# Linear attention on one core: q loaded, transposed and stored for two heads at a time, with fewer buffers and new instruction orders

## The chip, the cores and the metric

The kernel runs on one core of a Trainium2 chip. The core has five engines that run their own instruction streams and meet only at semaphores: TensorE (PE, matrix products and transposes), VectorE (DVE), ScalarE (ACT), GpSimd (POOL) and SyncE (SP), which here issues the transfers. Sixteen DMA engines move the data between memory and the on-chip SBUF; TensorE writes its results into PSUM. The metric is the time of one execution on the device in microseconds, lower is better. Before the change it is 169.24 us, the median of three runs (169.21 to 169.28).

## The reference

There are 32 heads; q, k and v of each are 2048 rows of 128 elements in bf16.

```python
phi_q = where(q > 0, q + 1, exp(q)) + 1e-6
phi_k = where(k > 0, k + 1, exp(k)) + 1e-6
kv  = einsum("bhsd,bhse->bhde", phi_k, v)      # 128 x 128 a head
z   = einsum("bhsd->bhd", phi_k)
num = einsum("bhqd,bhde->bhqe", phi_q, kv)
den = einsum("bhqd,bhd->bhq", phi_q, z) + 1e-6
out = num / den
```

Each head reads 1.5 MB and writes 0.5 MB, so the kernel moves 64 MB (67.1 million bytes).

## The kernel before

A head's 2048 rows lie on 128 partitions, 16 consecutive rows on each (`rows`, line 268). One load of q, k or v is therefore 128 partitions of 16 x 128 bf16 elements, 4,096 contiguous bytes a partition, 512 KB in all. The kernel keeps NI = 7 buffers each for k, q and v, and NO = 16 buffers for the output (line 14). A load may be issued when the operations that read its buffer for the head before (seven heads earlier) are done; the final scaling of a head may be written when the store of the head 16 before has landed.

The feature map is written as min(exp(x), 1) + 1e-6 plus max(x, 0), in two separate tensors that are summed by the matrix product. The steps of head h, by the names that the orders use:

- `ldk`, `ldq`, `ldv` (line 340): the loads, all on SP's queue but the first of v, which ACT issues.
- `ek` (ACT, line 366) and `em` (DVE clamp, line 344): min(exp(k), 1) + 1e-6. `rk` (POOL, line 351; DVE for the first heads): max(k, 0). `v1` (POOL, line 376; DVE at the start): v copied beside a column of ones.
- `kv` (PE, line 383): 32 products of 128 rows by 129 columns, the sum over all rows of the head; `kvs` (DVE, line 355) copies the result to SBUF.
- `T` (PE, line 393): 16 transposes of 128 by 128 into the one PSUM tile `xT`, in two halves. `eq` (ACT, line 397), `emq` (DVE, line 344), `rqa` (ACT, line 349, the first `NA[h]` of the 16 tiles) and `rqb` (DVE, line 350, the others): the same map for q, out of PSUM. The next head's T waits for all readers of `xT`.
- `n` (PE, lines 415 to 422): 32 products and a few small ones, numerator and denominator, in two groups (`n.0` 12 tiles, `n.1` 4 tiles). `a`, `r` (DVE, lines 435, 438) form the reciprocal, and `f` (DVE, line 442) scales group by group into an output buffer.
- `st` (SP, line 450): the store. For most heads it is one transfer of 128 partitions. The stores of head 12 (`ROWS`) and of head 14 (`HALF`) are split into unequal pieces by partitions, 51, 64 and 13, and 68, 60 and 128.

No loop sets the order at run time. The five lists in `ORDER` (lines 97 to 161) give, engine by engine, the order in which all steps of all heads stand; `Program.resolve` (line 199) derives from each step's dependencies the semaphore waits that are still needed. In the middle of the kernel PE's list repeats `kv(h) n(h-1).0 T(h+1) n(h-1).1`, ACT's repeats `ek(h+1) eq(h) rqa(h)`, and POOL does `rk` and `v1` of head h + 2 after `kv(h)`, since `rk`, `v1` and `em` have two buffers each. SP's list mixes loads and stores; SP issues strictly in that order, so a step that has to wait holds back everything behind it in the list. The transfers that are already issued go on meanwhile.

Of the kernel before, what the change touches and what calls it, by code (L numbers as in the profile page):

```python
# [6 lines left out]
P = 128  # L7
# [4 lines left out]
ON = {"rk0.0": "DVE", "rk0.1": "DVE", "rk1.0": "DVE", "v10.1": "DVE", "v11.0": "DVE", "rk2.0": "DVE", "v12.0":  # L12
      "DVE", "rk3.0": "DVE", "v13.0": "DVE"}
NI, NO, NE, NR, NV, NQ, NK = 7, 16, 2, 2, 2, 2, 2
WARM = (2, 8, 4, 1, 1, 1, 1, 1, 1, 1)
HALVES = ((0, 8), (8, 16))
WHOLE = ((0, 16),)

# [9 lines left out]
def ldk_parts(h):  # L28
    return WHOLE

# [12 lines left out]
NA = (8, 8, 8, 8, 8, 8, 8, 8, 8, 8, 8, 8, 8, 8, 8, 8, 8, 8, 8, 8, 8, 8, 8, 8, 8, 8, 8, 8, 8, 8, 14, 16)  # L43


def na(h):
    return NA[h] if h else 0

# [7 lines left out]
HALF = {14: ((0, 68), (68, 128))}  # L56
ROWS = {12: ((0, 51), (51, 115), (115, 128))}
# [29 lines left out]
def rqb_parts(h):  # L87
# [4 lines left out]
    if h == NH - 1:  # L92
# [6 lines left out]
        w3 w9 w7 T0.1 T0.0 w5 w2 w1 T1.0 T1.1 kv0.0 w0 kv0.1 w4 w8 w6 kv1.0 n0.0 T2.1 T2.0 n0.1 kv2.0 n1.0  # L99
        T3.1 n1.1 T3.0 kv3.0 n2.0 T4.1 n2.1 T4.0 kv4.0 n3.0 T5.1 n3.1 T5.0 kv5.0 n4.0 T6.1 T6.0 n4.1 kv6.0  # L100
        n5.0 T7.0 n5.1 T7.1 kv7.0 n6.0 T8.1 T8.0 n6.1 kv8.0 n7.0 T9.0 T9.1 n7.1 kv9.0 n8.0 T10.0 T10.1 n8.1
        kv10.0 n9.0 T11.0 T11.1 n9.1 kv11.0 n10.0 T12.0 T12.1 n10.1 kv12.0 n11.0 T13.0 T13.1 n11.1 kv13.0
        n12.0 T14.0 T14.1 n12.1 kv14.0 n13.0 T15.0 T15.1 n13.1 kv15.0 n14.0 T16.0 T16.1 n14.1 kv16.0 n15.0
        T17.0 T17.1 n15.1 kv17.0 n16.0 T18.0 T18.1 n16.1 kv18.0 n17.0 T19.0 T19.1 n17.1 kv19.0 n18.0 T20.0
        T20.1 n18.1 kv20.0 n19.0 T21.0 T21.1 n19.1 kv21.0 n20.0 T22.0 T22.1 n20.1 kv22.0 n21.0 T23.0 T23.1
        n21.1 kv23.0 n22.0 T24.1 T24.0 n22.1 kv24.0 n23.0 T25.1 T25.0 n23.1 kv25.0 n24.0 T26.0 T26.1 n24.1
        kv26.0 n25.0 T27.1 T27.0 n25.1 kv27.0 n26.0 T28.1 T28.0 n26.1 kv28.0 n27.0 T29.1 T29.0 n27.1 kv29.0
        n28.0 T30.0 T30.1 n28.1 kv30.0 n29.0 n29.1 T31.0 kv31.0 T31.1 n30.0 n30.1 n31.0 n31.2 n31.1
    """,
    "DVE": """  # L110
        ones rk0.0 rk0.1 rqb0.1 rqb0.0 v10.1 em0.0 v1ones0 v1ones1 eps0 em0.1 rk1.0 emq0.1 emq0.0 eps2 em1.0
        eps1 v11.0 kvs0 emq1.0 rqb1.0 rk2.0 v12.0 rk3.0 em2.0 r0.0 kvs1 f0.0 em3.0 v13.0 a0.1 kvs2 r0.1
        rqb2.0 f0.1 r1.0 f1.0 emq2.0 em4.0 a1.1 rqb3.0 r1.1 kvs3 f1.1 r2.0 f2.0 emq3.0 em5.0 a2.1 rqb4.0
        r2.1 kvs4 f2.1 r3.0 f3.0 emq4.0 em6.0 a3.1 r3.1 rqb5.0 f3.1 r4.0 kvs5 f4.0 emq5.0 em7.0 a4.1 rqb6.0
        r4.1 kvs6 f4.1 r5.0 f5.0 emq6.0 em8.0 a5.1 rqb7.0 r5.1 kvs7 f5.1 r6.0 f6.0 emq7.0 em9.0 a6.1 kvs8
        r6.1 rqb8.0 f6.1 r7.0 f7.0 emq8.0 em10.0 a7.1 rqb9.0 r7.1 f7.1 r8.0 kvs9 f8.0 emq9.0 em11.0 a8.1
        r8.1 rqb10.0 f8.1 r9.0 kvs10 f9.0 emq10.0 em12.0 a9.1 r9.1 rqb11.0 f9.1 r10.0 kvs11 f10.0 emq11.0
        em13.0 a10.1 r10.1 rqb12.0 f10.1 r11.0 kvs12 f11.0 emq12.0 em14.0 a11.1 r11.1 rqb13.0 f11.1 r12.0
        kvs13 f12.0 emq13.0 em15.0 a12.1 r12.1 rqb14.0 f12.1 r13.0 kvs14 f13.0 emq14.0 em16.0 a13.1 r13.1
        rqb15.0 f13.1 r14.0 kvs15 f14.0 emq15.0 em17.0 a14.1 r14.1 rqb16.0 f14.1 r15.0 kvs16 f15.0 emq16.0  # L120
        em18.0 a15.1 r15.1 rqb17.0 f15.1 r16.0 kvs17 f16.0 emq17.0 em19.0 a16.1 r16.1 rqb18.0 f16.1 r17.0
        kvs18 f17.0 emq18.0 em20.0 a17.1 r17.1 rqb19.0 f17.1 r18.0 kvs19 f18.0 emq19.0 em21.0 a18.1 r18.1
        rqb20.0 f18.1 r19.0 kvs20 f19.0 emq20.0 em22.0 a19.1 r19.1 rqb21.0 f19.1 r20.0 kvs21 f20.0 emq21.0
        em23.0 a20.1 r20.1 rqb22.0 f20.1 r21.0 kvs22 f21.0 emq22.0 em24.0 a21.1 rqb23.0 r21.1 kvs23 f21.1
        r22.0 f22.0 emq23.0 em25.0 a22.1 r22.1 rqb24.0 f22.1 r23.0 kvs24 f23.0 emq24.0 em26.0 a23.1 kvs25
        r23.1 rqb25.0 f23.1 r24.0 f24.0 emq25.0 em27.0 a24.1 rqb26.0 r24.1 f24.1 r25.0 kvs26 f25.0 emq26.0
        em28.0 a25.1 kvs27 r25.1 rqb27.0 f25.1 r26.0 f26.0 emq27.0 em29.0 a26.1 r26.1 rqb28.0 f26.1 r27.0
        kvs28 f27.0 emq28.0 em30.0 a27.1 r27.1 rqb29.0 f27.1 r28.0 kvs29 f28.0 emq29.0 a28.1 kvs30 r28.1
        f28.1 em31.0 rqb30.0 r29.0 emq30.0 f29.0 a29.1 kvs31 emq31.0 r29.1 f29.1 emq31.1 emq31.2 r30.0 f30.0
        a30.1 r30.1 f30.1 r31.2 r31.0 f31.2 a31.1 f31.0 r31.1 f31.1  # L130
    """,
    "ACT": """
        exp ldv0.0 ek0.1 eq0.1 eq0.0 ek0.0 ek1.0 eq1.0 ek2.0 rqa1 ek3.0 eq2.0 rqa2 ek4.0 eq3.0 rqa3 ek5.0
        eq4.0 rqa4 ek6.0 eq5.0 rqa5 ek7.0 eq6.0 rqa6 ek8.0 eq7.0 rqa7 ek9.0 eq8.0 rqa8 ek10.0 eq9.0 rqa9
        ek11.0 eq10.0 rqa10 ek12.0 eq11.0 rqa11 ek13.0 eq12.0 rqa12 ek14.0 eq13.0 rqa13 ek15.0 eq14.0 rqa14
        ek16.0 eq15.0 rqa15 ek17.0 eq16.0 rqa16 ek18.0 eq17.0 rqa17 ek19.0 eq18.0 rqa18 ek20.0 eq19.0 rqa19
        ek21.0 eq20.0 rqa20 ek22.0 eq21.0 rqa21 ek23.0 eq22.0 rqa22 ek24.0 eq23.0 rqa23 ek25.0 eq24.0 rqa24
        ek26.0 eq25.0 rqa25 ek27.0 eq26.0 rqa26 ek28.0 eq27.0 rqa27 ek29.0 eq28.0 rqa28 ek30.0 eq29.0 rqa29
        ek31.0 rqa30 eq30.0 eq31.0 eq31.1 eq31.2 rqa31
    """,  # L140
    "POOL": """
        ident0 ident v10.0 rk4.0 v14.0 rk5.0 v15.0 rk6.0 v16.0 rk7.0 v17.0 v18.0 rk8.0 rk9.0 v19.0 rk10.0
        v110.0 v111.0 rk11.0 v112.0 rk12.0 v113.0 rk13.0 v114.0 rk14.0 v115.0 rk15.0 v116.0 rk16.0 rk17.0
        v117.0 rk18.0 v118.0 v119.0 rk19.0 v120.0 rk20.0 rk21.0 v121.0 rk22.0 v122.0 v123.0 rk23.0 v124.0
        rk24.0 rk25.0 v125.0 rk26.0 v126.0 rk27.0 v127.0 rk28.0 v128.0 rk29.0 v129.0 rk30.0 v130.0 rk31.0
        v131.0
    """,
    "SP": """
        ldq0.0 ldk0.0 ldq1.0 ldk1.0 ldk3.0 ldv1.0 ldk2.0 ldv2.0 ldq2.0 ldv3.0 ldk4.0 ldq3.0 ldv4.0 ldk5.0
        ldq4.0 ldv5.0 ldq5.0 ldk6.0 ldk7.0 ldv6.0 ldq6.0 ldv7.0 ldq8.0 ldq7.0 ldv8.0 ldk8.0 ldk9.0 ldk11.0  # L150
        ldk10.0 ldv9.0 ldv10.0 ldq9.0 ldv14.0 ldq10.0 ldk13.0 ldv11.0 ldv12.0 ldq11.0 ldk12.0 ldq13.0
        ldk14.0 ldv13.0 ldq12.0 ldk15.0 ldq14.0 st1.0 ldk16.0 ldk18.0 ldv19.0 ldv15.0 ldq15.0 ldq16.0
        ldk17.0 ldq17.0 ldv16.0 ldk19.0 ldv18.0 ldv17.0 st3.0 ldk20.0 st0.0 ldq20.0 ldq21.0 ldq18.0 ldv20.0
        st12.0 ldk21.0 ldv21.0 st7.0 ldq19.0 ldk22.0 ldk23.0 st2.0 ldv23.0 ldq22.0 ldv22.0 ldk26.0 ldv25.0
        st4.0 ldv24.0 ldk25.0 ldq23.0 ldv26.0 ldk24.0 st5.0 st6.0 ldq27.0 ldq24.0 st10.0 ldk28.0 ldq25.0
        ldk27.0 st8.0 ldq26.0 ldq29.0 ldv27.0 st9.0 ldv28.0 ldk29.0 ldq28.0 st22.0 st12.2 ldv29.0 ldv30.0
        ldk30.0 st11.0 ldq30.0 st14.1 ldk31.0 st12.1 st15.0 ldv31.0 ldq31.0 st18.0 st13.0 st20.0 st14.2
        st17.0 st16.0 st14.0 st21.0 st26.0 st23.0 st27.0 st25.0 st24.0 st29.0 st19.0 st28.0 st30.0 st31.0
# [99 lines left out]
def bass_standalone__linear_attn_elu__prompt_kernel(nc: bass.Bass, q: bass.AP, k: bass.AP, v: bass.AP, out: bass.AP):  # L258
# [11 lines left out]
    with ExitStack() as es:  # L270
# [11 lines left out]
        k_sb, q_sb, v_sb = (sb([P, NI, NT, D]) for _ in range(3))  # L282
# [15 lines left out]

        def over(name, h, parts, t0, t1):
            return [f"{name}{h}.{i}" for i, (a, b) in enumerate(parts(h)) if a < t1 and t0 < b]  # L300
# [4 lines left out]
        def freed(n, h, *names):  # L305
            return [d for name, parts in names for d in every(name, h - n, parts)] if h >= n else []
# [4 lines left out]

        def rqs(h, t0=0, t1=NT):
            return ([f"rqa{h}"] if t0 < na(h) else []) + over("rqb", h, rqb_parts, t0, t1)
# [25 lines left out]
        def load(name, dst, src, h, i, t0, t1, last):  # L339
            add("ACT" if f"ld{name}{h}.{i}" in BY_ACT else "SP", f"ld{name}{h}.{i}", lambda e: e.dma_start(dst[:, h % NI, t0:t1], rows(src, h)[:, t0:t1]),  # L340
                last, dma=f"{name}{h % NI}.{i}")
# [15 lines left out]
        def head(h):  # L357
            for i, (a, b) in enumerate(ldk_parts(h)):
                load("k", k_sb, kf, h, i, a, b, freed(NI, h, ("ek", k_parts), ("rk", k_parts)))
            for i, (a, b) in enumerate(ld_parts(h)):  # L360
                load("q", q_sb, qf, h, i, a, b, freed(NI, h, ("T", t_parts)))
            for i, (a, b) in enumerate(ld_parts(h)):
                load("v", v_sb, vf, h, i, a, b, freed(NI, h, ("v1", v_parts)) if h else ["ident"])
# [133 lines left out]
```

## Time and profile before

| | before |
|---|---|
| median of three runs | 169.24 us |
| the profiled execution: its own time | 169.41 us |
| its span, first to last instruction | 168.1 us |
| granted TensorE clock | 0.988 |
| PE, DVE, ACT, POOL busy | 155.7, 155.8, 149.4, 84.4 us |
| read from memory, written to memory | 50.33 MB, 16.78 MB |
| mean DMA rate over the span | 402 GB/s |

The busy time of an engine is the sum over its instructions, with overlaps counted once; matrix products and the weight loads that overlap them (PEld) are counted apart. The span is shorter than the execution's own time, which has start and end around it (1.31 us in this execution). The slices divide the span into 40 parts of 4.2 us; a digit 9 is 90% or more. The DMA share is the mean over the sixteen DMA engines; as their packets overlap a little, it can pass 1.

### The profile page before, as it was taken

What the parts mean: (1) busy time and instruction counts of PE and PEld (TensorE: products, weight loads), DVE (VectorE), ACT (ScalarE), POOL (GpSimd) and SP (SyncE); (2) the same over time, 40 slices, a digit from 0 to 9 for tenths busy, and PEclk for the clock granted to TensorE, in tenths of its full rate; (3) what the DMA queues carried; (4) which work ended last, traced back from release to release, by engine and by line L of the source; (5) the groups of instructions that cost most, each with busy time, mean ns of one, the idle gap of its engine ahead of it and who ended that gap; (6) DMA issues with size and microseconds to landing.
All of it is one profiled execution on the core that took longest, in us unless ns stands there. A gap on an engine that the chain in (4) does not pass through costs nothing.

```text
span 168.1 us, 6169 instructions
## 1 busy us (share of the span) xinstructions
PE 155.7 (93%) x2709; PEld 150.8 (90%) x2709; DVE 155.8 (93%) x309; ACT 149.4 (89%) x101; POOL 84.4 (50%) x63
## 2 busy tenths in 40 slices
PE   3999999999999999999599999999999999999650
PEld 1689999999999999999589999999999999999640
DVE  0499999999999999999999999999999999999971
ACT  3799999999999999999669999999999999997600
POOL 1100355566666666546926667676555566670000
PEclk9999999999999999999999999999999999999995
DMA  5999999999999999999999999999999999999996
GB/s 212 409 420 414 401 407 411 401 409 406 407 409 403 408 411 417 407 406 416 406 421 414 418 412 408 421 412 416 414 415 416 414 417 411 415 415 414 375 406 243
DMA packets 18910, 67.51 MB, mean 402 GB/s; under 512 B 2115, under 2 KB 2499, under 8 KB 18883
## 3 DMA queue, kind: packets, MB, share of 16 engines
q1 hardware_dynamic: 18739, 66.59, 98.6%
q8 instruction: 21, 0.34, 0.8%
q10 hardware_dynamic: 144, 0.52, 0.8%
q14 instruction: 6, 0.05, 0.1%
HBM read 50.33 MB, written 16.78 MB: 399 GB/s over the span
## 4 chain that ended last, share of the span: by engine, by line
DVE 52%; PE 40%; DMA 2%; ACT 2%; issue 1%; SPq 0%
DVE la L442 24%; PE la L383 16%; DVE la L344 14%; PE la L420 9%; PE la L422 8%; PE la L393 7%; DVE la L350 7%; DVE la L438 3%; DMA la<-in_k_dram 2%; DVE la L355 2%; ACT la L397 1%; DVE la L376 1%; DVE la L435 1%; ACT la L366 1%; PE la L415 0%
## 5 line engine op out<-in xcount | busy, mean ns | idle before, releaser
L442 DVE TENSOR_TENSOR la<-la 128x1536 bf16<-128x1536 f32 (+2 forms) x65 | 78.0, 1200 | 0.6
L351 POOL TENSOR_SCALAR la<-la 128x2048 bf16<-128x2048 bf16 x28 | 54.1, 1935 | 38.2 <-PE la L383 38.2
L420 PE MATMUL la<-la 128*128 128x129 bf16 x512 | 67.0, 219 | 0.3 <-DVE la L355 0.3
L422 PE MATMUL la<-la 128*128 128x129 bf16 x512 | 67.0, 219 | 0.0
L397 ACT ACTIVATE la<-la 128x2048 bf16<-128x2048 bf16 (+2 forms) x35 | 60.3, 1729 | 5.9 <-PE la L422 2.9
L366 ACT ACTIVATE la<-la 128x2048 bf16<-128x2048 bf16 (+1 forms) x33 | 61.4, 1860 | 3.3 <-DMA la<-in_k_dram 3.2
L383 PE MATMUL la<-la 128*128 128x129 bf16 x1024 | 63.4, 220 | 0.0
L383 PEld LDWEIGHTS la<-la 128*128 128x128 bf16 x1024 | 59.4, 98 | 0.7 <-DVE la L355 0.5
L422 PEld LDWEIGHTS la<-la 128*128 128x128 bf16 x512 | 49.6, 97 | 0.0
L420 PEld LDWEIGHTS la<-la 128*128 128x128 bf16 x512 | 47.9, 97 | 0.5 <-DVE la L355 0.4
L344 DVE TENSOR_SCALAR la<-la 128x2048 bf16<-128x2048 bf16 (+2 forms) x68 | 44.9, 697 | 0.0
L376 POOL COPY la<-la 128x1024 int32<-128x1024 int32 (+1 forms) x29 | 30.7, 1058 | 26.9 <-PE la L383 16.6
L393 PE MATMUL la<-la 128*128 128x128 bf16 x512 | 35.6, 222 | 2.2 <-DMA la<-in_q_dram 1.1
L393 PEld LDWEIGHTS la<-la 128*128 128x128 bf16 x512 | 30.8, 99 | 3.5 <-DMA la<-in_q_dram 2.0
L349 ACT ACTIVATE la<-la 128x1024 bf16<-128x1024 bf16 (+2 forms) x31 | 33.1, 1067 | 0.0
L350 DVE TENSOR_SCALAR la<-la 128x1024 bf16<-128x1024 bf16 (+2 forms) x37 | 23.7, 646 | 5.7 <-DMA la<-in_k_dram 4.3
L415 PE MATMUL la<-la 128*128 128x3 bf16 (+1 forms) x128 | 21.6, 168 | 2.7 <-DVE la L442 1.7
L415 PEld LDWEIGHTS la<-la 128*128 128x128 bf16 x128 | 12.5, 98 | 3.2 <-DVE la L442 2.1
L438 DVE RECIPROCAL la<-la 128x12 f32<-128x12 f32 (+2 forms) x65 | 12.8, 199 | 1.4 <-PE la L422 0.8
L355 DVE CAST la<-la 128x129 bf16<-128x129 f32 x32 | 8.0, 251 | 0.0
L331 PE MATMUL la<-la 128*128 128x480 bf16 x21 | 6.3, 441 | 1.5 <-POOL la L316 1.5
L331 PEld LDWEIGHTS la<-la 128*128 128x128 bf16 x21 | 2.2, 114 | 3.5 <-POOL la L316 1.5
(15 smaller groups left out, 10.3 us busy)
## 6 DMA issues: line engine op xcount, KB each, us to landing
la<-in_q_dram SPq DMA_DIRECT2D x32, 512.0 KB, 14.8
la<-in_k_dram SPq DMA_DIRECT2D x32, 512.0 KB, 14.8
la<-in_v_dram SPq DMA_DIRECT2D x31, 512.0 KB, 14.5
out_dram<-la SPq DMA_DIRECT2D x29, 512.0 KB, 14.0
la<-in_v_dram ACTq DMA_DIRECT2D x1, 512.0 KB, 5.8
out_dram<-la SPq DMA_DIRECT2D x2, 256.0 KB
out_dram<-la SPq DMA_DIRECT2D x2, 192.0 KB, 3.1
out_dram<-la SPq DMA_DIRECT2D x1, 204.0 KB
```

The source lines that it names most:

```text
L344: add(on(key, "DVE"), key, lambda e: e.tensor_scalar(t, t, 1.0, EPS, op0=ALU.min, op1=ALU.add), deps)
L349: "ACT": lambda e: e.activation(dst, src, ACT.Relu),
L350: "DVE": lambda e: e.tensor_scalar(dst, src, 0.0, None, op0=ALU.max),
L351: "POOL": lambda e: e.tensor_scalar(dst, src, BIG, 0.0, op0=ALU.min, op1=ALU.max)}[eng], deps)
L366: add("ACT", f"ek{h}.{i}", lambda e, a=a, b=b: e.activation(em_sb[:, h % NE, a:b], k_sb[:, h % NI, a:b], ACT.Exp), over("ldk", h, ldk_part ...
L383: ins = e.matmul(kv_ps, lhsT=src[:, j], rhs=v1_sb[:, h % NV, j, 0:NC], start=(j + part == 0), stop=(j == NT - 1 and part == 1))
L393: ins = e.transpose(xT[:, j], q_sb[:, h % NI, j], ident[:])
L397: add("ACT", f"eq{h}.{i}", lambda e, a=a, b=b: e.activation(emq_sb[:, h % NQ, a:b], xT[:, a:b], ACT.Exp), over("T", h, t_parts, a, b) + fr ...
L415: e.matmul(_ap(o_ps[:, :], o + D, [[NC, m]]), lhsT=ones[:], rhs=epsr[:, 0:m], start=True, stop=False, skip_group_check=True)
L420: e.matmul(to, lhsT=emq_sb[:, h % NQ, t], rhs=kvs_sb[:, h % NK, 0:NC], start=late and c == 0, stop=False, skip_group_check=True)
L422: ins = e.matmul(to, lhsT=rq_sb[:, h % NQ, t], rhs=kvs_sb[:, h % NK, 0:NC], start=False, stop=True, skip_group_check=True)
L442: return e.tensor_tensor(out=_ap(o_sb[:, :, :, :], first(o_sb[:, h % NO, t0, 0:1]) - first(o_sb[:, :, :, :]), [[m * D, nb], [D, m], [1, D] ...
```

## The change

For heads 4 to 27 q is handled in pairs (4 and 5, 6 and 7, and so on):

- Load: one transfer fetches q of both heads into two neighbouring buffers. A partition now holds 32 consecutive rows, 8,192 contiguous bytes; partitions 0 to 63 hold the first head, 64 to 127 the second. Twelve transfers of 1 MB replace 24 of 512 KB.
- Transpose: T of the first head of a pair takes the first 16 row slots of every partition, T of the second the other 16, so each transposes tiles in which 64 columns belong to one head and 64 to the other.
- `eq`, `rqa`, `rqb` and `emq` write and read their SBUF tiles as runs of 64 elements, so that the tile of one head for one product is 128 contiguous columns again. n of both heads of a pair needs the T, `eq` and the rest of both. To hold this, NQ is 4 and no longer 2.
- Output: partition 64 b + r of the output buffer holds rows 32 r + 16 b + j of the head. A pair is stored by two transfers that each write both heads: the first from partitions 0 to 63, the second from 64 to 127, each with 4,096 bytes a partition and head, 512 KB in all. Both need the scaling of both heads to be done, and both output buffers come free when both have landed.
- Buffers: k, q and v have 6 each (7 before), the output has 14 (16 before).
- The splits of stores by partitions move from heads 12 and 14 to heads 2 and 3.
- All five orders are new. T stands one head further ahead of kv in PE's list from head 5 on (`kv(h) n(h-1).0 T(h+2) n(h-1).1`), back to one ahead for heads 30 and 31. ACT's list is `ek(h) eq(h) rqa(h)`. `rk5` and `v10.0` go from POOL to DVE, `v13` from DVE to POOL. `NA` differs at heads 1, 2, 5, 29 and 30. In SP's list stores begin earlier, and 14 of them (with the three parts of the last counted as one) stand behind the last load.

The code also has a second switch for pairs of k and v (`KFIRST`, `KLAST`), which is off, and books who uses which buffer (`fill`, `used`) in place of `freed`.

```diff
-ON = {"rk0.0": "DVE", "rk0.1": "DVE", "rk1.0": "DVE", "v10.1": "DVE", "v11.0": "DVE", "rk2.0": "DVE", "v12.0":
-      "DVE", "rk3.0": "DVE", "v13.0": "DVE"}
-NI, NO, NE, NR, NV, NQ, NK = 7, 16, 2, 2, 2, 2, 2
+ON = {"rk0.0": "DVE", "rk0.1": "DVE", "v10.1": "DVE", "rk1.0": "DVE", "v11.0": "DVE", "rk2.0": "DVE", "v12.0":
+      "DVE", "rk3.0": "DVE", "v10.0": "DVE", "rk5.0": "DVE"}
+NI = {"k": 6, "q": 6, "v": 6}
+NO, NE, NR, NV, NQ, NK = 14, 2, 2, 2, 4, 2
+QFIRST, QLAST = 4, 28
+KFIRST, KLAST = 0, 0
...
+def pair(h):
+    return QFIRST <= h < QLAST
...
-NA = (8, 8, 8, 8, 8, 8, 8, 8, 8, 8, 8, 8, 8, 8, 8, 8, 8, 8, 8, 8, 8, 8, 8, 8, 8, 8, 8, 8, 8, 8, 14, 16)
+NA = (8, 0, 6, 8, 8, 0, 8, 8, 8, 8, 8, 8, 8, 8, 8, 8, 8, 8, 8, 8, 8, 8, 8, 8, 8, 8, 8, 8, 8, 14, 16, 16)
...
-HALF = {14: ((0, 68), (68, 128))}
-ROWS = {12: ((0, 51), (51, 115), (115, 128))}
+HALF = {3: ((0, 68), (68, 128))}
+ROWS = {2: ((0, 51), (51, 115), (115, 128))}
...
     "PE": """
+        w9 w2 w4 T0.0 T0.1 w1 kv0.0 w0 w7 T1.1 T1.0 kv0.1 w3 w6 w5 w8 kv1.0 n0.0 T2.1 T2.0 kv2.0 n0.1 n1.0
+        T3.0 T3.1 n1.1 kv3.0 T4.1 T4.0 n2.0 n2.1 T5.1 T5.0 kv4.0 n3.0 n3.1 T6.0 T6.1 kv5.0 n4.0 T7.0 T7.1
+        n4.1 kv6.0 n5.0 T8.1 T8.0 n5.1 kv7.0 n6.0 T9.0 T9.1 kv8.0 n6.1 n7.0 T10.0 n7.1 T10.1 kv9.0 n8.0
+        T11.0 T11.1 n8.1 kv10.0 n9.0 T12.0 T12.1 n9.1 kv11.0 n10.0 T13.0 T13.1 n10.1 kv12.0 n11.0 T14.0
+        T27.0 T27.1 n24.1 kv26.0 n25.0 T28.1 T28.0 n25.1 kv27.0 n26.0 T29.0 T29.1 n26.1 kv28.0 n27.0 n27.1
+        kv29.0 n28.0 T30.0 T30.1 n28.1 kv30.0 n29.0 n29.1 T31.0 T31.1 kv31.0 n30.0 n30.1 n31.0 n31.1 n31.2
...
+        ones rk0.0 em0.0 v1ones0 rk0.1 v10.1 eps0 eps1 v1ones1 em0.1 v10.0 rk1.0 rqb0.1 rqb0.0 emq0.1 emq0.0
+        em1.0 v11.0 eps2 kvs0 rk2.0 v12.0 emq1.0 rqb1.0 em2.0 kvs1 r0.0 f0.0 rk3.0 em3.0 a0.1 kvs2 r0.1
+        rqb2.0 f0.1 r1.0 f1.0 em4.0 rqb3.0 a1.1 emq2.0 rk5.0 r1.1 kvs3 f1.1 emq3.0 rqb4.0 r2.0 emq4.0 f2.0
+        em5.0 a2.1 r2.1 kvs4 f2.1 rqb5.0 r3.0 f3.0 emq5.0 em6.0 a3.1 rqb6.0 r3.1 f3.1 r4.0 kvs5 f4.0 em7.0
...
+        ident0 ident rk4.0 v13.0 v14.0 rk6.0 v15.0 v16.0 rk7.0 v17.0 rk8.0 v18.0 v19.0 rk9.0 rk10.0 v110.0
+        v111.0 rk11.0 v112.0 rk12.0 v113.0 rk13.0 v114.0 rk14.0 v115.0 rk15.0 v116.0 rk16.0 rk17.0 v117.0
+        rk25.0 v125.0 rk26.0 v126.0 v127.0 rk27.0 rk28.0 v128.0 v129.0 rk29.0 v130.0 rk30.0 v131.0 rk31.0
...
+        ldq0.0 ldk0.0 ldk1.0 ldq1.0 ldk2.0 ldv1.0 ldv2.0 ldk3.0 ldq2.0 ldk4.0 ldq3.0 ldv3.0 ldq4.0 ldk5.0
+        ldv6.0 ldv4.0 ldk6.0 ldv5.0 ldq6.0 ldq8.0 ldk7.0 ldv7.0 ldk8.0 ldk9.0 ldv9.0 ldv8.0 st3.0 ldv10.0
+        ldq10.0 ldk12.0 ldk10.0 ldk11.0 ldv11.0 ldv13.0 st2.2 ldk13.0 ldk15.0 ldq12.0 ldv12.0 ldv16.0
...
+        ldv26.0 st11.0 st8.0 ldk26.0 ldv27.0 ldq26.0 ldq28.0 st10.0 st15.0 ldk27.0 ldk28.0 ldk29.0 ldq29.0
+        ldv28.0 ldv29.0 st12.0 st13.0 ldv31.0 ldk30.0 ldv30.0 ldk31.0 st14.0 ldq30.0 st17.0 st25.0 ldq31.0
+        st16.0 st24.0 st20.0 st23.0 st21.0 st18.0 st28.0 st19.0 st27.0 st22.0 st29.0 st26.0 st30.0 st31.0
...
-        k_sb, q_sb, v_sb = (sb([P, NI, NT, D]) for _ in range(3))
+        k_sb, q_sb, v_sb = (sb([P, NI[x], NT, D]) for x in "kqv")
...
+        def fill(buf, n, heads, key):
+            slots = [(buf, h % n) for h in heads]
+            for s, h in zip(slots, heads):
+                if users.get(s, (None, None, None))[0] != h:
+                    users[s] = (h, users[s][2] if s in users else [], [])
+            return [d for s in slots for d in users[s][1]]
+
+        def used(buf, n, heads, key):
+            for h in heads:
+                u = users[buf, h % n]
+                assert u[0] == h, (buf, h, u[0])
+                u[2].append(key)
...
+            two = both(h, kpair if name != "q" else pair)
+            if len(two) == 1:
+                to, at = dst[:, h % ni, t0:t1], rows(src, h)[:, t0:t1]
+            elif name == "q":
+                to = dst[:, h % ni:h % ni + 2].rearrange("p h j d -> p (h j) d")
+                at = src[h:h + 2].rearrange("h (p j) d -> (h p) j d", j=2 * NT)
+            else:
+                to, at = dst[:, h % ni:h % ni + 2], src[h:h + 2].rearrange("h (p j) d -> p h j d", j=NT)
+            last = fill(name, ni, two, key) + (["ident"] if key in BY_ACT else [])
+            add("ACT" if key in BY_ACT else "SP", key, lambda e: e.dma_start(to, at), last,
+                dma=f"{name}{h % ni}.{i}")
...
+                        src = q_sb[:, h0 % NI["q"] + (blk * NT + j) // NT, j] if len(two) == 2 else q_sb[:, h % NI["q"], j]
+                        ins = e.transpose(xT[:, j], src, ident[:])
                     return ins
-                add("PE", f"T{h}.{i}", g, over("ldq", h, ld_parts, a, b) + ["ident"] + (over("eq", h - 1, q_parts, a, b) + rqs(h - 1, a, b) if h else []))
+                key = f"T{h}.{i}"
+                add("PE", key, g, [f"ldq{h0}.0"] + ["ident"] + (eqs(h - 1, a, b) if h else []))
+                used("q", NI["q"], two, key)
+            if len(two) == 2:
+                def part(buf, a, b):
+                    pairs = buf[:, h0 % NQ:h0 % NQ + 2].rearrange("p h j d -> p (h j d)")
+                    return pairs.rearrange("p (j h b r) -> p j h b r", j=NT, h=2, b=2)[:, a:b, :, blk]
+
+                def src(a, b):
+                    return xT[:, a:b].rearrange("p j (h r) -> p j h r", h=2)
...
+            def tile(buf, t):
+                if len(two) == 1:
+                    return buf[:, h % NQ, t]
+                return buf[:, h0 % NQ:h0 % NQ + 2].rearrange("p h j d -> p (h j d)")[:, (2 * t + blk) * P:(2 * t + blk + 1) * P]
...
+            elif blk:
+                for c in range(2):
+                    key = f"st{h0 + c}.0"
+                    add("SP", key, lambda e, c=c: e.dma_start(
+                        of[h0:h0 + 2].rearrange("h (r b j) d -> b r h (j d)", b=2, j=NT)[c],
+                        o_sb[64 * c:64 * c + 64, h0 % NO:h0 % NO + 2].rearrange("p h j d -> p h (j d)")),
+                        [d for x in two for d in every("f", x, groups)], dma=f"o{(h0 + c) % NO}")
+                    used("o", NO, two, key)
...
```

## The prediction

> **What bounds the kernel now.** I read the slices of the page first, then busy time by stages, then the chain of waits, then the one place where the slices show a dip.
>
> ```profile
> PE   3999999999999999999599999999999999999650
> DVE  0499999999999999999999999999999999999971
> DMA  5999999999999999999999999999999999999996
> q1 hardware_dynamic: 18739, 66.59, 98.6%
> out_dram<-la SPq DMA_DIRECT2D x29, 512.0 KB, 14.0
> ```
>
> PE, DVE and the DMA engines are all at 9 nearly throughout. Who is really full is told by rates, in the table by stages (busy time and instructions of PE, PEld, DVE, ACT, POOL, then clock, DMA share, GB/s):
>
> ```profile
> 20.00:78.00 58.00, 58.00 (x1057) 57.92 (x1055) 57.55 (x113) 57.50 (x39) 35.50 (x25) 1.00 1.03 408
> 78.00:86.00 8.00, 5.76 (x99) 5.25 (x97) 7.96 (x10) 5.21 (x4) 5.75 (x4) 1.00 1.03 416
> 86.00:150.00 64.00, 64.00 (x1168) 63.98 (x1166) 63.51 (x127) 63.56 (x42) 41.24 (x28) 1.00 1.03 415
> 155.00:160.00 5.00, 3.38 (x62) 3.20 (x59) 4.93 (x11) 3.12 (x4) 0.00 (x0) 1.00 0.95 382
> 160.00:168.00 8.00, 2.26 (x36) 1.91 (x36) 3.82 (x10) 0.00 (x0) 0.00 (x0) 0.76 0.82 326
> ```
>
> A head is 84 instructions on PE (32 kv, 16 T, 32 n, 4 small), so 64.00 x 84 / 1168 = 4.60 us. It is 2.10 MB for the DMA engines, 5.06 us at 415 GB/s. The DMA engines are therefore the slower side: 128 transfers of 512 KB at 1.275 us (landings in the trace follow each other by 1.25 to 1.28) are 163.2 us, and they run from about 2.7 us on. The engines keep ahead by putting stores off. Only behind 155 us does the DMA share fall: there the last heads' results are awaited, and the last store, issued at 164.7, lands with the span's end, 3.4 us later. Both paths end together. On the compute path the chain of waits shows a head's period and one flaw:
>
> ```profile
> 74.11 1.20 DVE la L344 x2
> 78.71 4.14 DVE la L344 x2
> 108.39 1.81 PE la L383 x32
> 113.00 1.81 PE la L383 x32
> ```
>
> The period is 113.00 - 108.39 = 4.61. Two clamps that take 1.20 took 4.14, 2.9 more. The timeline of POOL and DVE there:
>
> ```profile
> 77.12 1.04 POOL L376 COPY la<-la 128x1024 int32<-128x1024 int32 x1 [3.66 <-PE la L393]
> 78.12 4.19 POOL L351 TENSOR_SCALAR la<-la 128x2048 bf16<-128x2048 bf16 x2
> 78.63 4.22 DVE L344 TENSOR_SCALAR la<-la 128x2048 bf16<-128x2048 bf16 x2
> ```
>
> v16 had landed at 77.0 in the trace, 1.9 us after kv14 had ended and POOL was due; v1 and two rk then ran into the clamps, which waited. So a load 1.9 us late cost 2.9 us.
>
> **The change, part by part.** Durations are of the profiled execution (169.41 us, span 168.1); the median of the runs is 0.17 lower, so a span s stands for a median of s + 1.14.
>
> *8 KB packets.* The trace's packet records show 159 ns for 4,096 bytes, 84 for 2,048 and 46 for 1,024: 9 ns of each do not scale. The 8,192-byte packets there belong to instruction fetches, and took 309 at the shortest, 329 in the median. The 12 pair loads bring each DMA engine 12 x 8 = 96 packets of 8 KB for 192 of 4 KB: at 309 a gain of 96 x 9 = 0.86 us, at 329 a loss of 96 x 11 = 1.06. I take 309, because three of them took exactly that and it continues the three other sizes. DMA path: 168.1 - 0.9 = 167.2.
>
> *Half-partition stores.* The 24 stores of pairs touch 64 partitions each, with the same packets (4 partitions x 2 heads x 4 KB on each of 16 engines). The nearest row is the piece of before's head 14 with partitions 68 to 127: its 60 packets of 2,048 bytes took 84 ns like those of the 128-partition piece, though up to five engines were in it at once. I take 0. The far end is that two engines share one way and a store takes twice 1.275: +1.275 each.
>
> [...]
>
> *Runs of 64 elements.* DVE's copy into runs of 128 elements took 687 ns, as much as the contiguous one of the same size, so I take 0 for emq, rqb and eq. The far end for DVE is the rate out of PSUM: 653 for 1,024 elements against 422, so some 0.46 a clamp, 24 x 0.46 = 11 us. ACT has no such row; it is busy 63.56 of 64 us, so each 1% of its two q passes (1.88 and 1.02) would cost 24 x 0.03 = 0.7 us.
>
> *DVE at the start.* Ahead of f2.0 DVE's list gains rk5, emq3, emq4 (0.60 each in the chain of waits), rqb4 (0.58), larger rqb1 and rqb2 (0.66), v10.0 (0.34) and loses v13 (0.60): +2.8. DVE has no gap there, so f2.0, which ended at 27.8, ends at 30.6. Then em5, a2.1, r2.1, kvs4, f2.1 (1.5) and rqb5, now over 16 tiles (1.1), let T6 (0.9) start at 33.2 and kv5 at 34.2; before, kv5 started at 31.5. Of these 2.7 us, 0.9 is T done a head earlier, given back at heads 29 to 31. Net +1.8.
>
> *The stall at 78.* Its cause, v16 late, is gone: v16 now stands 41st in SP's list, lands near 60, and POOL wants it at 79. -2.9.
>
> *The end.* DVE's list behind f28.0 lacks rqb30 (0.2). f31.1 ended at 164.7; 164.7 - 2.9 + 1.8 - 0.2 = 163.4. With 3.4 to land, 166.8.
>
> *Fewer buffers.* A transfer waits some 14 us in the queue (14.0 to 14.8 on the page), eleven transfers deep. Five buffers fewer are 5 x 1.275 = 6.4 us at most, so the DMA engines are not left idle. SP waits more: st3.0 stands 27th, waits for f3.0 (about 35), and holds all loads behind it; its queue lasts to about 41, which hides that.
>
> *Loads closer to their use.* Counted in units of 1.275 (2.48 for a pair), k27 lands at 125.5 on the first engine. One transfer's landings in before are spread by 3.7 to 4.8 us over the engines in that stretch, so it is whole at 129.2 to 130.3. kv25 ends at 34.2 + 20 x 4.62 + 2.0 = 128.6, v127 takes 1.04, so rk27 wants it at 129.6: up to 0.7 late. v30, whole at 143.1, is wanted when kv28 ends, 142.5. The same engine lateness moves both, so I count it once: 0.6, with 0 and a whole collision (2.9) as ends. Compute path: 166.8 + 0.6 = 167.4.
>
> The compute path ends last, by 0.2 over the DMA path: span 167.4, median 168.5.
>
> **The rivals.**
>
> *Late loads collide (slower).* Mechanism: k27 or v30 reaches POOL late, POOL's rk runs into DVE's clamps as at 78, and PE waits. For it: slack under 1 us at those two, also at v12, k20 and q26, where before's list had mostly 3 us and more behind 40 us. Against it: everything behind one stall has more slack. It decides from 168.1 - 166.8 = 1.3 us of stalls on; one full collision gives 166.8 + 2.9 = 169.7, median 170.8, two give 173.7.
>
> [...]
>
> *Half-partition stores take twice as long (slower).* The DMA path is the longer side, so it pays in full: 167.2 + 30.6 = 197.8, median about 199; a tenth of the effect (3 us) gives 171.3. Against it are the 84 ns packets. [...]
>
> *No gain (same).* If an 8 KB run goes as two packets of 4 KB, the DMA path stays at 168.1, median 169.2. For it: no 8 KB packet of a load is in the trace.
>
> **How the numbers follow.** Under 0.2% (0.34 us) a measurement of this kernel can hardly tell from no change. The forecast, with its neighbours up to 168.9, gets 0.48: two independent sums agree on it within 0.2 us, but the margin to before is only 0.7. Late loads get 0.27, half-partition stores and strided passes 0.13, no gain 0.12. Hence faster 0.48, same 0.12, slower 0.40. The forecast's own range is 167.4 (no lateness, and the idle DMA time behind 155 used) to 168.9; to hold 8 in 10 the range goes past one collision to 172.2 and leaves out two collisions and most of the slow stores.
>
> **What would show it.** Right: packets of 8,192 bytes of 309 ns, the DMA share at 1.03 to 155 us; no clamp pair over 2 us; kv5 near 34.2; f31.1 near 164. Wrong: store packets over 159 ns or a lower GB/s with stores in flight; clamps of the q side over 0.7 us or an ACT period over 4.62; gaps of PE before T or kv behind 85 us with a late load; a DVE wait for an output buffer, of which there are 14.

## The result: 6.9% slower, and the profile after

The changed kernel took 180.88 us in the median of four runs (180.46 to 181.88), the kernel before 169.23 beside it: a ratio of 1.0692, interval 1.0666 to 1.0719. The forecast was 168.5, its range ended at 172.2. The profiled run took 180.66 us with a span of 179.4; before's span was 168.1. Medians and ranges here are of all runs of a kernel; a ratio and its interval leave out a run over 1.5% above the fastest of its kernel, which is one run each of two kernels below (182.68 and 178.78 us).

The slices of the changed kernel's page, with the row of its DMA queue and of its whole stores and pair loads:

```profile
PE   6589997899999999999999999999995999994000
DVE  0499999999999999999999999999989999999200
DMA  6999999999999999999999999999999999999995
GB/s 234 408 422 410 412 408 420 407 407 420 405 418 400 420 407 407 371 388 410 418 422 417 408 407 396 387 409 417 417 409 419 395 336 338 253 249 262 253 249 215
q1 hardware_dynamic: 17011, 66.59, 97.3%
out_dram<-la SPq DMA_DIRECT2D x29, 512.0 KB, 13.0
la<-in_q_dram SPq DMA_DIRECT2D x12, 1024.0 KB, 14.1
```

Before's row of rates, for comparison:

```profile
GB/s 212 409 420 414 401 407 411 401 409 406 407 409 403 408 411 417 407 406 416 406 421 414 418 412 408 421 412 416 414 415 416 414 417 411 415 415 414 375 406 243
```

The DMA row is at 9 to the end, as before's was; the bytes are the same 66.59 MB. But the GB/s row falls in the last eight slices, from about 410 to 337 in two of them and then to about 250, while the DMA engines are nearly as busy: each transfer takes longer. PE and DVE stop some three slices ahead of the end. The same in the table by stages (columns as in the prediction):

```profile
20.00:104.00 84.00, 82.38 (x1488) 81.59 (x1486) 83.35 (x164) 80.50 (x54) 51.01 (x36) 1.00 1.02 408
104.00:120.00 16.00, 16.00 (x294) 16.00 (x292) 15.90 (x30) 15.66 (x11) 9.70 (x8) 1.00 1.02 399
120.00:150.00 30.00, 27.78 (x501) 27.31 (x499) 28.86 (x55) 26.71 (x18) 17.68 (x12) 1.00 1.00 397
150.00:160.00 10.00, 10.00 (x185) 9.95 (x183) 9.56 (x22) 8.47 (x7) 3.13 (x2) 1.00 0.98 264
160.00:168.00 8.00, 3.49 (x61) 3.08 (x58) 6.54 (x13) 0.86 (x1) 0.00 (x0) 1.00 0.96 255
168.00:179.00 11.00, 0.00 (x0) 0.00 (x0) 0.00 (x0) 0.00 (x0) 0.00 (x0) 0.51 0.84 251
```

Up to 150 us the table shows little: 408, 399 and 397 GB/s, against 408 to 416 in before; the first low slice begins at 143.5 us. From 150 on nearly only stores are left (the last load, q31, is whole at 152.6). f31.1 ends at 166.91, before's at 164.70; the last store lands 12.4 us after it, before's 3.4. So of the 11.3 us of span, 9.0 are stores still queued when the compute has ended (12.4 - 3.4), and 2.2 are a later end of compute. The trace's packet records say what kind of slowness it is: in 150 to 160 us the store packets of 4,096 bytes took 272 ns in the median and 314 at the ninth decile; 159 is the undisturbed value. In that stretch 52% of the packets took over 250 ns and 43% at most 165; in before's trace 0.3% took over 250.

Most of the later end of compute is one place in the chain of waits:

```profile
114.05 0.99 SPq L543
115.08 1.28 SPq L543
116.40 15.81 DMA la<-in_k_dram
132.29 1.92 ACT la L410
134.23 3.01 DVE la L386 x2
138.23 1.07 PE la L445 x16
```

k27, issued behind two half-partition stores (L543), is whole at 132.2, ACT starts on it at 132.29, and DVE's two clamps, which run into POOL's rk27, take 3.01 instead of 1.2. The next transposes start at 138.23, after PE had idled for some 2 us. It is the stall that the prediction named at k27, larger than its 0.6. With the store of whole rows below, PE was busy all through that stage:

```profile
120.00:150.00 30.00, 30.00 (x549) 29.97 (x547) 29.45 (x60) 28.74 (x20) 20.43 (x14) 1.00 1.03 415
```

### The profile page after: what moved, and what is told of

Read it like the earlier page. It is cut to its first block, busy times and chain, and to the rows that moved or that the text cites. A ratio compares the mean times of both kernels' runs of the same rounds, so it can differ in the third digit from the quotient of the medians.

```text
span 179.4 us, 6127 instructions
## 1 busy us (share of the span) xinstructions
PE 155.6 (87%) x2709; PEld 150.2 (84%) x2709; DVE 157.2 (88%) x309; ACT 146.8 (82%) x99; POOL 82.4 (46%) x62
## 3 DMA queue, kind: packets, MB, share of 16 engines
q1 hardware_dynamic: 17011, 66.59, 97.3%
## 4 chain that ended last, share of the span: by engine, by line
PE 58%; DVE 18%; DMA 13%; ACT 1%; SPq 1%; issue 0%; ACTq 0%
PE la L430 23%; PE la L500 12%; PE la L445 12%; PE la L502 11%; DMA la<-in_k_dram 9%; DVE la L526 6%; DVE la L386 5%; DVE la L392 5%; DMA la<-in_v_dram 4%; SPq L543 1%; DVE la L422 1%; ACT la L410 1%; DVE la L522 1%; DVE la L397 1%; ACT L355 0%
## 5 line engine op out<-in xcount | busy, mean ns | idle before, releaser
L526 DVE TENSOR_TENSOR la<-la 128x1536 bf16<-128x1536 f32 (+1 forms) x65 | 77.9, 1199 | 0.7
L393 POOL TENSOR_SCALAR la<-la 128x2048 bf16<-128x2048 bf16 x27 | 52.0, 1925 | 42.0 <-PE la L430 40.9
L430 PEld LDWEIGHTS la<-la 128*128 128x128 bf16 x1024 | 59.3, 98 | 3.6 <-DVE la L422 3.0
L502 PEld LDWEIGHTS la<-la 128*128 128x128 bf16 x512 | 49.6, 97 | 0.0
L500 PEld LDWEIGHTS la<-la 128*128 128x128 bf16 x512 | 47.9, 97 | 0.3 <-DVE la L526 0.2
L422 POOL COPY la<-la 128x1024 int32<-128x1024 int32 x29 | 30.8, 1062 | 28.2 <-PE la L430 21.2
L445 PE MATMUL la<-la 128*128 128x128 bf16 x512 | 34.2, 220 | 3.7 <-DVE la L392 3.4
L445 PEld LDWEIGHTS la<-la 128*128 128x128 bf16 x512 | 30.0, 98 | 5.5 <-DVE la L392 4.2
L391 ACT ACTIVATE la<-la 128x1024 bf16<-128x1024 bf16 (+3 forms) x29 | 31.9, 1099 | 0.0
L392 DVE TENSOR_SCALAR la<-la 128x1024 bf16<-128x1024 bf16 (+3 forms) x37 | 24.9, 677 | 4.2 <-DMA la<-in_k_dram 4.2
L495 PEld LDWEIGHTS la<-la 128*128 128x128 bf16 x128 | 12.5, 98 | 1.8 <-DVE la L526 1.8
L522 DVE RECIPROCAL la<-la 128x12 f32<-128x12 f32 (+1 forms) x65 | 12.9, 199 | 1.3 <-PE la L502 0.5
L519 DVE TENSOR_SCALAR la<-la 128x4 f32<-128x4 f32 (+1 forms) x32 | 5.0, 157 | 0.3 <-PE la L430 0.2
```

Of the source, the lines that this page charges most:

```text
L392: "DVE": lambda e: e.tensor_scalar(dst, src, 0.0, None, op0=ALU.max),
L393: "POOL": lambda e: e.tensor_scalar(dst, src, BIG, 0.0, op0=ALU.min, op1=ALU.max)}[eng], deps)
L422: add(on(key, "POOL"), key, lambda e, a=a, b=b, word=word: e.tensor_copy(v1_sb[:, h % NV, a:b, 0:D].bitcast(word), v_sb[:, h % NI["v"], a: ...
L430: ins = e.matmul(kv_ps, lhsT=src[:, j], rhs=v1_sb[:, h % NV, j, 0:NC], start=(j + part == 0), stop=(j == NT - 1 and part == 1))
L445: ins = e.transpose(xT[:, j], src, ident[:])
L495: e.matmul(_ap(o_ps[:, :], o + D, [[NC, m]]), lhsT=ones[:], rhs=epsr[:, 0:m], start=True, stop=False, skip_group_check=True)
```

## The experiments

The theory (A), to be tested: the store of a pair reads 64 neighbouring partitions, which have half of the ways out of SBUF; many such stores in a row take up to twice as long, few of them among other transfers little. The ways are the author's supposition, and no trace shows them; what the runs can show is how long stores of such partitions take. The rivals: (B) the scattered 4 KB runs on the DRAM side are slow; (C) 8 KB loads, new orders and fewer buffers are; (D) late loads are. Times of before stand beside each group, from the same chip.

### Three other stores, and half stores in the kernel before

The pair's store replaced by one of 128 partitions:

```
-  of[h0:h0 + 2].rearrange("h (r b j) d -> b r h (j d)", b=2, j=NT)[c],
-  o_sb[64 * c:64 * c + 64, h0 % NO:h0 % NO + 2].rearrange("p h j d -> p h (j d)")),
+  rows(of, h0 + c), o_sb[:, (h0 + c) % NO]),
```

> The 24 stores of pairs write 128 partitions of one output buffer each into that head's rows, 512 KB as before, with the same waits for both heads and the same places in SP's list (the rows of heads 4 to 27 come out in another order). Theory A (a store of 64 partitions has half the way out of SBUF): the stores behind the last load land 1.25 to 1.4 us apart instead of 1.7 to 2.6; the end goes back to f31.1 plus 3.4, with f31.1 at 165 to 167, so 170 to 171.5 us in the median. Rival B (the scattered 4 KB runs in DRAM are slow): 170 to 171.5 too. Rival C (8 KB loads, orders, fewer buffers): stays at 180 to 181. Rival D (late loads, k27 above all): the two microseconds of that stall alone are in question, so 180 too.

Measured: 168.57 us (168.39 to 168.72), before 169.35; ratio 0.9957, interval 0.9942 to 0.9972. The tail is gone, and so is the stall at k27; that is why the time lies below the 170 to 171.5 that A had given.

The half-partition store with another DRAM side:

```
-  of[h0:h0 + 2].rearrange("h (r b j) d -> b r h (j d)", b=2, j=NT)[c],
+  of[h0 + c].rearrange("(h r j) d -> r h (j d)", h=2, j=NT),
```

> The stores of pairs still read 64 partitions of two output buffers, but each writes one head's 512 KB in one piece, 4 KB runs one behind the other in DRAM (the rows of heads 4 to 27 come out in another order). A: stays at 180 to 181, with 4 KB packets of stores far over 159 ns in the tail. B: the DRAM side was the cost, so 170 to 171.5. C and D: stays at 180 to 181.

Measured: 181.62 us (179.78 to 182.68), before 169.35; ratio 1.0693, interval 1.062 to 1.0765: no different from the changed kernel (1.0692).

A whole store with the changed kernel's DRAM side:

```
+  of[h0:h0 + 2].rearrange("h (r b j) d -> b (h r) (j d)", b=2, j=NT)[c],
+  o_sb[:, (h0 + c) % NO].rearrange("p j d -> p (j d)")),
```

> The stores of pairs read 128 partitions of one output buffer, but write the same 4 KB runs, every second one of two heads, that the changed kernel's stores write (rows of heads 4 to 27 in another order). A: like the store of whole rows, 170 to 171.5. B: stays at 180 to 181. C and D: 180 to 181.

Measured: 169.57 us (168.91 to 170.31), before 169.35; ratio 1.0009, interval 0.9991 to 1.0026. Its stage from 150 to 160 us, where the changed kernel had 264 GB/s:

```profile
150.00:160.00 10.00, 8.51 (x153) 8.15 (x151) 9.44 (x22) 6.65 (x6) 0.15 (x1) 1.00 1.00 405
```

With the changed kernel these three make a square: 64 partitions are slow with either DRAM side, 128 fast with either. B is worth some 1.0 us by the medians (169.57 against 168.57). C falls as a cause of the large loss, since the loads, orders and buffers stayed; D falls too, since the late load went away with the half stores.

The same cause put into the kernel before, and nothing else:

```
+SPLIT = (16, 17, 18, 20, 21, 23, 24, 25, 26, 27)
-  for i, (a, b, x, y) in enumerate(st_parts(h)):
+  for i, a, b, x, y in ([(0, 0, NT, 0, 64), (9, 0, NT, 64, P)] if h in SPLIT else ...):
-  ldq31.0 st18.0 st13.0 st20.0 st14.2 st17.0 st16.0 st14.0 st21.0 st26.0 ...
+  ldq31.0 st18.0 st20.0 st18.9 st20.9 st13.0 st14.2 st17.0 st16.0 st17.9 st16.9 st14.0 ...
```

> The kernel before, with ten of the stores behind its last load (heads 16, 17, 18, 20, 21, 23 to 27) cut into a piece of partitions 0 to 63 and one of 64 to 127, two heads' first pieces ahead of their second ones; nothing else changes. A: ten stores at about 2.2 us instead of 1.275 are 9 us more, less some 2 us of idle DMA time in that tail: 175 to 179 us. B, C, D: 512 KB take as long in two pieces, so 169.2 to 170.

Measured: 174.94 us (173.94 to 175.67), before 169.35; ratio 1.033, interval 1.0289 to 1.0371, just under the 175 to 179 that A gave. The tail in the tables by stage, first of the changed kernel with whole rows, then of the kernel before, then of this run:

```profile
150.00:160.00 10.00, 8.51 (x153) 8.16 (x151) 9.44 (x22) 6.64 (x6) 0.15 (x1) 1.00 1.00 405
160.00:168.00 8.00, 1.75 (x33) 1.57 (x30) 3.53 (x8) 0.00 (x0) 0.00 (x0) 0.84 0.73 287
```

```profile
147.00:155.00 8.00, 8.00 (x149) 7.97 (x146) 7.61 (x18) 7.18 (x6) 2.97 (x2) 1.00 1.03 415
155.00:160.00 5.00, 3.38 (x62) 3.20 (x59) 4.93 (x11) 3.12 (x4) 0.00 (x0) 1.00 0.95 382
```

```profile
147.00:155.00 8.00, 7.93 (x141) 7.65 (x138) 7.54 (x17) 5.94 (x5) 1.51 (x2) 1.00 0.97 327
155.00:160.00 5.00, 2.01 (x34) 1.83 (x34) 3.37 (x8) 2.64 (x3) 0.00 (x0) 1.00 0.82 259
160.00:168.00 8.00, 2.26 (x36) 1.92 (x36) 3.86 (x11) 0.00 (x0) 0.00 (x0) 0.89 0.90 277
```

405 GB/s where stores are whole; 327 and 259 in before's own program as soon as its late stores are cut in halves, where it had 415 and 382. (The 287 behind 160 is in part waiting for the last results: the DMA share is 0.73. So is some of the 259, at a share of 0.82; the 327, at 0.97, is not.) The loads, the buffers, the size of the packets and all orders but that of these stores are before's, so the half partition is enough by itself.

### Is it 64 partitions, or 64 neighbours?

The same ten stores of the kernel before, again in two pieces each, now of even and of odd partitions:

```
-  rows(of, h)[x:y, a:b], o_sb[x:y, h % NO, a:b]),
+  rows(of, h)[x // 64:P:2, a:b] if h in SPLIT else rows(of, h)[x:y, a:b],
+  o_sb[x // 64:P:2, h % NO, a:b] if h in SPLIT else o_sb[x:y, h % NO, a:b]),
```

> The kernel before with the ten stores behind the last load cut into two pieces as in the run of 174.9 us, but of even and of odd partitions instead of lower and upper ones. Theory A in its narrow form (the way out of SBUF belongs to neighbouring partitions, and lower 64 use half of the ways): pieces of even partitions reach all ways, so 169.2 to 170. Rival (64 partitions are slow whichever they are, or two pieces cost by being two): 174 to 176.

Measured: 169.39 us (169.22 to 170.19), before 169.33; ratio 1.0004 (0.9995 to 1.0014). Its tail:

```profile
147.00:155.00 8.00, 8.00 (x148) 7.97 (x146) 7.64 (x17) 5.95 (x5) 1.67 (x2) 1.00 1.02 406
155.00:160.00 5.00, 3.23 (x59) 2.88 (x57) 4.29 (x10) 2.78 (x3) 0.00 (x0) 1.00 0.97 385
```

406 and 385 GB/s with pieces of the same count, size and order. So neither the number of partitions nor the number of pieces costs; which partitions they are does. The two runs stand at 174.94 us with lower and upper pieces and at 169.39 with even and odd ones; they try two ways of taking 64 partitions and no others.

### The same stores among loads

Eight early stores of the kernel before in halves, the late ones whole:

```
+SPLIT = (0, 2, 3, 5, 6, 7, 8, 10)
-  st3.0 ldk20.0 st0.0 ...  st5.0 st6.0 ldq27.0 ...
+  st3.0 st0.0 ldk20.0 st3.9 st0.9 ...  st5.0 st6.0 st5.9 st6.9 ldq27.0 ...
   ... (and the same two pieces a store as above)
```

> The kernel before with eight stores that stand among loads (heads 0, 2, 3, 5, 6, 7, 8, 10) cut into pieces of partitions 0 to 63 and 64 to 127, two heads' lower pieces at one place and their upper pieces at another; the stores behind the last load stay whole. If a half-partition store is mostly hidden among loads (some 0.14 us each by the packets over 159 ns there): 169.3 to 170.5 us. If it costs 0.9 us each wherever it stands: 7 us more, 175 to 177.

Measured: 170.42 us (169.87 to 170.68), before 169.33; ratio 1.0059, interval 1.0043 to 1.0074: 1.1 us for eight stores, 0.14 each, against 0.56 each for the ten in the tail (174.94 - 169.35 = 5.6 us, net of the idle DMA time that before's tail had to give). Almost no packet of that trace is long: from 104 to 147 us 0.5% of the 4 KB packets took over 250 ns, where before had 0.3%. The loss shows in the last landings. Those of one transfer lay 3.6 us apart over the 16 engines ahead of the four halves of heads 5 and 6, and 4.6 us behind them, and a single packet at 114.7 us, of 1,065 ns where 159 is usual, would account for nearly all of that step if it was the last engine's. The trace with whole rows has such a packet too (1,256 ns at 143.1 us), so what made it long is not shown; the small loss itself is, as all four runs lie above all of before's (169.08 to 169.56).

The changed kernel with pairs up to head 15 alone, so that its tail has whole stores only:

```
-QFIRST, QLAST = 4, 28
+QFIRST, QLAST = 4, 16
-  ldq16.0
+  ldq16.0 ldq17.0        (likewise 18 to 26)
```

> Only heads 4 to 15 are loaded as pairs; q of heads 16 to 27 comes as two plain loads at the pair's place, and their stores write 128 partitions each, so that every store behind the last load is a whole one, while the half-partition stores that stand among loads stay. Theory A, with half-partition stores costing 9 us in the tail and little among loads: the tail is gone, and the end is f31.1 plus 3.4; f31.1 lies between 163.9 (no stall at k27) and 166.9 (the stall stays), so 168.5 to 171.5 us. Rival A2 (the halves cost as much among the loads, and the tail only shows what was put off): at least 11 of the 24 stores still pay 0.9 us each, 10 us in all, so 178 to 180.

Measured: 171.31 us (171.07 to 171.64), before 169.38; ratio 1.0118 (1.0099 to 1.0138). Of the 11.65 us (180.88 - 169.23) 9.7 are gone with the late half stores. What is left is a stall, at v23 this time. POOL and then DVE in its timeline:

```profile
113.98 1.04 POOL L422 COPY la<-la 128x1024 int32<-128x1024 int32 x1 [1.34 <-DMA la<-in_v_dram]
115.37 1.95 POOL L393 TENSOR_SCALAR la<-la 128x2048 bf16<-128x2048 bf16 x1 [0.35 <-PE la L430]
```

```profile
114.23 3.63 DVE L386 TENSOR_SCALAR la<-la 128x2048 bf16<-128x2048 bf16 x2
```

POOL waited 1.34 us for v23, its two instructions then fell on the clamps, and these took 3.63 instead of 1.2: the collision of before at 78 us again, in another place. f31.1 ended at 165.88, 2.3 later than with whole rows (163.56).

The same with k27's load ahead of four loads and three stores:

```
-  ldv26.0 st11.0 st8.0 ldk26.0 ldv27.0 ldq26.0 ldq27.0 ldq28.0 st10.0 st15.0 ldk27.0 ldk28.0
+  ldv26.0 st11.0 ldk26.0 ldk27.0 ldv27.0 ldq26.0 ldq27.0 st8.0 ldq28.0 ldk28.0 st10.0 st15.0
```

> The same, with k27's load moved ahead by three loads and three stores in SP's list (st8, st10 and st15 go behind it). If the stall at k27 is a late load and costs 2 us at the end: 1.5 to 2 us less than the kernel it is made from where that still stalls, else the same to 0.3; 168.5 to 169.7 us. If f31.1 does not set the end, no change.

Measured: 174.70 us (174.22 to 175.34), 3.4 us more instead of less. The edit made a wait of its own. DVE's timeline:

```profile
122.33 0.23 DVE L397 CAST la<-la 128x129 bf16<-128x129 f32 x1
128.05 1.76 DVE L526 TENSOR_TENSOR la<-la 128x1536 bf16<-128x1536 f32 x1 [5.48 <-issue]
```

st8 landed at 127.97 there; f22.0 writes the output buffer that st8 empties (22 - 14 = 8) and started at 128.05 after 5.48 us without work. With 14 buffers st8 could not be put off by five loads. The edit was also aimed at the wrong load, as the kernel that it is made from stalls at v23; the run says nothing on k27.

### Can the order of the late stores mend it?

One lower store, one upper store in turn:

```
-  st16.0 st24.0 st20.0 st23.0 st21.0 st18.0 st28.0 st19.0 st27.0 st22.0 st29.0 st26.0
+  st16.0 st21.0 st20.0 st23.0 st18.0 st19.0 st28.0 st24.0 st27.0 st22.0 st29.0 st26.0
```

> The changed kernel with its pair stores behind the last load in another order: one of partitions 0 to 63, then one of 64 to 127, in turn. A, with the DMA engines up to 5 us apart from each other, so that both halves are in work at once: some of the loss comes back, 174 to 179 us; if the engines go in step, 180 to 181. If the loss were in each store by itself (DRAM side, packet size): 180 to 181.

Measured: 177.25 us (175.87 to 178.78), before 169.38; ratio 1.0435, interval 1.0377 to 1.0493.

Pieces of one head, lower and upper in turn:

```
+FINE = (16, 18, 19, 20, 21, 22, 23, 24, 26, 27)
-  st16.0 st24.0 st20.0 st23.0 ...
+  st16.0 st21.0 st16.9 st21.9 st20.0 st23.0 st20.9 st23.9 ...
   ... (and each of these ten stores issued as two, one head at a time)
```

> The changed kernel with ten of those stores cut into two pieces of 256 KB (64 partitions, one head), pieces of the lower and the upper partitions in turn. A: both halves are in work at once nearly always, and most of the 9 us come back: 171 to 175 us. If the engines go in step even so: 180 to 181. If more and smaller transfers cost by themselves: 181 or more.

Measured: 177.26 us (175.69 to 177.6), before 169.38; ratio 1.0445, interval 1.0396 to 1.0495. Against the 1.0692 of the changed kernel both bring back some 4 of the 11.65 us, as A lets expect where the engines are some microseconds apart (one transfer's landings lay 3.7 to 4.8 us apart over the engines in before's trace). The finer mixture brings no more, where I had expected 171 to 175; why it doesn't was not settled.

### What the rest of the change is worth

The kernel with whole rows, with its pair load in 4 KB runs:

```
-  to = dst[:, h % ni:h % ni + 2].rearrange("p h j d -> p (h j) d")
-  at = src[h:h + 2].rearrange("h (p j) d -> (h p) j d", j=2 * NT)
+  to, at = dst[:, h % ni:h % ni + 2], src[h:h + 2].rearrange("h (p j) d -> p h j d", j=NT)
```

> The kernel with whole-row stores of the pairs, with one thing more changed: the pair load fetches its 1 MB as 4 KB runs, two a partition, instead of 8 KB runs (which rows of q meet in a buffer changes with it). If the DMA engines set the end and an 8 KB packet saves 9 ns (309 against twice 159): 12 x 8 x 9 ns = 0.86 us more than that kernel, so 169.2 to 169.6 us. If the compute path sets the end there: no change, 168.4 to 168.8.

Measured: 169.06 us in the median of twelve runs (168.79 to 170.59, most within 169.3), ratio to before 1.0002, interval 0.9982 to 1.0022, where whole rows had 0.9957 (0.9942 to 0.9972). By the medians the 8 KB packets are worth 0.49 us, between the two answers that were expected.

The changed kernel without pairs:

```
-QFIRST, QLAST = 4, 28
+QFIRST, QLAST = 4, 4
-  ldq4.0
+  ldq4.0 ldq5.0        (likewise 6 to 26)
```

> The changed kernel without pairs: its orders, buffer counts and places in every list, but q of each head loaded by itself (two plain loads at the pair's place) and every store whole and after its own head alone. If 8 KB packets are worth their 0.86 us: 169.0 to 169.6 us, about as before. If the new orders alone carry the gain of the whole-row kernel: 168.4 to 168.8. If the stall at k27 or v23 comes without half-partition stores too: 170 or more.

Measured: 169.05 us (168.85 to 169.22), before 169.33; ratio 0.9984 (0.9975 to 0.9992). It computes what before does, with every row in its place, and is the fastest such version here: 0.16% ahead of before, less than the 0.2% that I had set as a difference to speak of, though the interval leaves out 1.

## Why the prediction was wrong, by its own steps

**Half-partition stores: the step that failed.** It cost them at 0, with 30.6 us as the far end (24 times 1.275), by the piece of 60 partitions in before's trace whose packets took 84 ns like all others. No run shows the 30.6, nor the shared way that it supposes: two fifths of it came, 180.88 against 168.57 us with whole rows, 12.3 us, and in the tail about half of the store packets took near twice their time (52% over 250 ns, 314 at the ninth decile, where 159 is usual). The row was true and misled all the same. It was a lone piece of 120 KB with at most six or seven of its packets under way at once (the prediction counted five engines). What the change does is another case: fourteen stores in a row behind the last load, ten of them half ones, with the DMA share at 0.96 to 0.98 until 168 us, so nearly all 16 engines were in stores. The question to ask of the row was how many engines draw on those partitions at one time. That this is what sets the two cases apart is argued: no run varied the number of engines alone. The prediction also had the other fact in hand: "The engines keep ahead by putting stores off", so the stores of the pairs gather where nothing but stores is left. Its rival "half-partition stores take twice as long" had the cause and no term for where the stores stand; 0.56 us each in a row against 0.14 among loads is that term for the halved stores of the kernel before, and in the changed kernel the 9.0 us of tail over ten stores are 0.9 each.

**Loads closer to their use** was right in place and way (k27, POOL's rk into the clamps, PE waiting) and wrong in cause. With whole rows k27 is whole at 129.64, within the 129.2 to 130.3 of the prediction, and nothing stalls. Behind half-partition stores it came at 132.21. A late k27 does not always collide: in the run with pieces of one head in turn it came at 131.82, the next pairs of clamps took 1.29 us, and f31.1 ended at 164.92. The rival *late loads collide* thus happened, as a consequence: f31.1 was 3.4 us later than with whole rows (166.91 against 163.56). In the changed kernel the tail covers that; with pairs to head 15 it set the end.

**The other terms held.** With whole rows f31.1 ended at 163.56 where the sum said 163.4, the span was 167.3 (167.4 predicted), the time 168.57 (168.5). That the last two agree so closely is in part luck: the 0.6 for late loads did not come, and the last store landed 3.7 us behind f31.1 instead of 3.4. *Runs of 64 elements* cost nothing: the ACT group that holds the strided passes, and the clamps, in the rows of the run with whole rows,

```profile
L465 ACT ACTIVATE la<-la 128x2048 bf16<-128x2048 bf16 (+2 forms) x35 | 60.3, 1731 | 6.4 <-PE la L445 4.7
L386 DVE TENSOR_SCALAR la<-la 128x2048 bf16<-128x2048 bf16 (+2 forms) x68 | 41.9, 653 | 0.7 <-ACT la L410 0.7
```

are at 1731 ns, where before had 1729, and at 653 (697 in before, where the collision at 78 is in the mean). *8 KB packets*: 1,536 of them with whole rows, median 309 ns as taken (though of the twelve in before's trace, which the choice rested on, the shortest took 307 and two took 309), mean 314.2 against twice 161.8, so 0.90 us of DMA time; half of it, 0.49, arrived at the end. q31's last landing came 0.52 earlier than with 4 KB runs. Where the other 0.4 us went is open. *The stall at 78* is gone. *DVE at the start* was too low for the changed kernel: kv5 at 35.3 instead of 34.2 (34.8 with whole rows). That f31.1 with whole rows met the sum all the same is luck of the same kind: what made up the 0.6 us is open.

**The chances.** Slower had 0.40, the cause that came a part of 0.13, which it shared with the strided passes. The range to 172.2 had room for one collision and a tenth of the store effect, which is where one unsuited row had put it.

## What to carry to other kernels

Before a transfer of fewer than 128 partitions is costed, ask whether it stands among other transfers or in a row of its like, with the DMA engines full of them (a share of 0.96 to 0.98 in the changed kernel): here a half-partition store cost 0.14 us in the first place and 0.56 to 0.9 in the second. Stores that are put off gather behind the last load, so the shape of a store is priced there. If half of the partitions must be stored, take every second one and not a block of neighbours (169.39 against 174.94 us); in the changed kernel the columns' order (b, r) forbids that, and a version with both 8 KB loads and even partitions was not tried.

## What the runs showed of the hardware

- 512 KB in two pieces of even and odd partitions goes at full rate (169.39 against 169.33 us), in pieces of 0 to 63 and 64 to 127 it doesn't (174.94). In that run 23% of the packets of 4,096 bytes from 150 to 160 us took over 250 ns, about twice the usual 159 (314 at the ninth decile); in the changed kernel 52% did, and the rate there was 264 GB/s where whole stores had 405.
- The DRAM side hardly matters: runs of 4 KB at a stride of 8 KB cost some 1.0 us in 24 stores (169.57 against 168.57).
- A lag between the DMA engines stayed, once there. In the run with early halves the spread of a transfer's landings went from 3.6 to 4.6 us at 113 to 117 us and kept at 4.6 to 4.7 until 131; the last load, 30 us later, was still 0.5 us later than in the kernel before (147.71 against 147.17).
- An 8 KB run of a load goes as one packet, of 309 ns in the median (1,536 packets for 12 MB).
